# Reordering the steps of a fused attention and token mixer: scores first, weights by casting loads, output weights issued later

## The chip, the cores and the metric

The kernel runs on one core of one Trainium2 chip. The metric is the device time of one execution in microseconds. The kernel before takes 103.31 us (median of three runs, 102.93 to 103.32). The profile's span, from the first to the last instruction, is shorter than the device time of the same run by 1.75 to 3.17 us in the fast runs of the record. Runs over 1.5% above the fastest of the same kernel are called slow and are left out of all comparisons of times.

## The reference

A retention-like attention, block by block with a decaying state, feeds a mixer that works along the sequence. B, H, S, D are 4, 8, 768, 64, the model width is 512, the mixer's inner width 64.

```python
for b in range(nb):                                   # blocks of 64 rows
    intra = np.einsum('bhic,bhjc->bhij', qb, kb) * Dmask[None]
    intra = np.einsum('bhij,bhjd->bhid', intra, vb)
    inter = np.einsum('bhid,bhde->bhie', qb * lam_pow[None], kv_state)
    out[:, :, sl] = intra + inter
    kv_state = lam_block[...] * kv_state + np.einsum('bhsd,bhse->bhde', kb * rev_pow, vb)
...
x = attn_out.transpose(0, 2, 1, 3).reshape(B, S, H * D)
wq, wk = x @ w_q, x @ w_k
mixed = np.einsum('bst,btd->bsd', np.einsum('bsd,btd->bst', wq, wk) / 8, x)
return np.maximum(mixed, 0.0) @ w_out
```

## The kernel before

The work is cut into 16 pairs (a batch and two of its heads), and the main loop has one step per pair. In the text, "the q turn of pair 9" is the group of twelve PE transposes that brings q of pair 9 into the form for the scores. The groups on PE are: q turn, k turn, scores (tile sc), states (tile dps, they need the V scaled by GpSimd, tile vn), inter (tile oa from gs, the copy of the states), values (tile oa from pr), flip (tile xp), and the mixer's wk, wq, py, pm and po. pm multiplies by Y, ScalarE's (ACT's) copy of py; po multiplies by the output weights, wo, and makes the output. In the traces PE's groups run in the program's order.

All loads but the first few and the mixer's small weights are cast from f32 to bf16 by the DMA and are issued by GpSimd, which also scales the V tiles. One pair's loads are these:

```python
def load_more(n):
    load_q(n)                                   # nc.gpsimd.dma_start
    load_kv(n, "k")
    scale_v(n - 2, nc.gpsimd) if n - 2 > 3 else None
    load_kv(n, "v")
...
    load_q(5)
    load_kv(5, "k")
    scale_v(3, nc.gpsimd)
    load_kv(5, "v")
    nc.gpsimd.dma_start(out=wo, in_=moe_w_out.rearrange("(kt p) j -> p kt j", p=128))
    load_more(6)
    load_more(7)
    make_dq(1)
    for n in range(N):
        if 8 <= n + 6 < N:
            load_more(n + 6)
```

So GpSimd's stream holds the output weights (512 KB in bf16) between the loads of pairs 5 and 6. Inside the loop PE's order is:

```python
        if n >= 1 and not (b >= 1 and kk >= 2):
            inter(n - 1)
            scores(n)
        elif n >= 1:
            mix_pm(p, [2 * kk - 4])
            scores(n)
            inter(n - 1)
            mix_pm(p, [2 * kk - 3])
        ...
        masks(n, 0)
        masks(n, 1)
        if n == 4 or n >= 8:
            back()                              # values, flip, po, wk
        if n <= 8:
            states(n)
        ...
        if n <= 8:
            turn(n + 1)                         # q turn, then k turn
        if 8 <= n < N - 1:
            states(n + 1)
```

Of the kernel before, what the change touches and what calls it, by code (L numbers as in the profile page):

```python
# [11 lines left out]
F32 = mybir.dt.float32  # L12
# [7 lines left out]
DHY = 64  # L20
NP = H // 2
# [6 lines left out]
def kernel(  # L28
# [62 lines left out]
    nc.sync.dma_start(out=k0, in_=kv_rows(0, k))  # L91
    q0 = consts.tile([128, 2, 3, 2 * D], F32, name="q0")
    nc.sync.dma_start(out=q0, in_=q_rows(0))
    wqk_f = consts.tile([128, 2, 4, DHY], F32, name="wqk_f")


    nc.scalar.preload_act_table_set("natural_log_exp_and_others")
# [72 lines left out]
    def make_dq(kk):  # L170
        nc.scalar.activation(out=Dq[kk], in_=ET, func=ACT.Exp, scale=lncol[:, kk : kk + 1])
# [5 lines left out]
    wo = consts.tile([128, 4, HD], BF16, name="wo")  # L177

    def load_wqk():

        nc.vector.memset(wqk_f[:, :, 0, 0:1], 0.0)
        for i, w in enumerate((moe_w_q, moe_w_k)):
            nc.sync.dma_start(out=wqk_f[:, i], in_=w.rearrange("(kt p) j -> p kt j", p=128))


    L = defaultdict(dict)
# [2 lines left out]
    def scale_v(n, eng):  # L189
        b, kk = pairs[n]  # L190
        vn = nat.tile([128, 2, NCH, D], BF16, tag="vn", name="vn")
        eng.tensor_tensor(  # L192
            out=vn,
            in0=staged.pop((n, "v")),
            in1=DvI[:, 2 * kk : 2 * kk + 2, :].unsqueeze(3).to_broadcast([128, 2, NCH, D]),
            op=ALU.mult,
        )
        L[n]["vn"] = vn
# [8 lines left out]
    def turn(n):  # L207
        turn_q(n)
        turn_k(n)
# [22 lines left out]
    def turn_k(n):  # L232
        L[n]["kn"] = kn = staged.pop((n, "k"))
        trk = pst([128, S], BF16, "trk")
        for c in range(NCH):
            for hl in range(2):
                nc.tensor.transpose(  # L237
                    trk[hl * 64 : hl * 64 + 64, c * CH : (c + 1) * CH], kn[:, hl, c, :], ident
                )
        kT = tsb.tile([128, S], BF16, tag="kT", name="kT")  # L240
        nc.scalar.copy(out=kT, in_=trk)  # L241
        L[n]["kT"] = kT
# [4 lines left out]
    def states(n):  # L247

        kn, vn = L[n]["kn"], L[n]["vn"]
        dps = pst([128, NCH - 1, D], F32, "dps")  # L250
        for c in range(NCH - 1):
            end = 2 if c < 2 else NCH - 1
            for hl in range(2):
                nc.tensor.matmul(  # L254
                    dps[hl * 64 : hl * 64 + 64, c:end, :],
                    kn[:, hl, c, :],
                    vn[:, hl, c, :].unsqueeze(1).to_broadcast([128, end - c, D]),
                    start=(c == 0),
                    stop=(c == NCH - 2),
                    skip_group_check=True,  # L260
                )
        gs = gsp.tile([128, NCH - 1, D], BF16, tag="gs", name="gs")
        two = gsp.tile([128, 1, D], F32, tag="two", name="two")
        nc.vector.tensor_copy(out=two, in_=dps[:, 1:2, :])
        nc.vector.tensor_copy(out=gs[:, 0:2, :], in_=dps[:, 0:2, :])
        nc.vector.tensor_tensor(
            out=gs[:, 2:, :],
            in0=dps[:, 2:, :],
            in1=two.to_broadcast([128, NCH - 3, D]),
            op=ALU.add,  # L270
        )
        L[n]["gs"] = gs

    def scores(n):
        kT = L[n]["kT"]
        sc = {}
        for a in range(2):
            for hl in range(2):
                sc[a, hl] = pst([128, 3, CH], F32, f"sc{hl}")
            for cc in range(3):  # L280
                c = 3 * a + cc
                for hl in range(2):
                    r = slice(hl * 64, hl * 64 + 64)
                    nc.tensor.matmul(  # L284
                        sc[a, hl][:, cc, :],
                        kT[r, c * CH : (c + 1) * CH],
                        qchunk(n, r, c),
                        start=True,
                        stop=True,
                        skip_group_check=True,  # L290
                    )
        L[n].update(sc=sc, pr={})

    def masks(n, a):
        for hl in range(2):
            t = prb.tile([128, 3, CH], BF16, tag="pr", name="pr")
            nc.vector.tensor_tensor(out=t, in0=L[n]["sc"][a, hl], in1=maskc, op=ALU.mult)  # L297
            L[n]["pr"][a, hl] = t

    def inter(n):  # L300

        gs = L[n]["gs"]
        oa = [pst([128, NCH, D], F32, "oa") for hl in range(2)]
        for c in range(1, NCH):
            for hl in range(2):
                r = slice(hl * 64, hl * 64 + 64)
                nc.tensor.matmul(
                    oa[hl][:, c, :],
                    qchunk(n, r, c),
                    gs[r, c - 1, :],  # L310
                    start=(c == 1),
                    stop=False,
                    skip_group_check=True,
                )
        L[n]["oa"] = oa
# [24 lines left out]
    def flip(n, eng=None):  # L340
        b, kk = pairs[n]
        xp = pst([128, NCH, CH], BF16, "xp")
        for t in range(NCH):
            nc.tensor.transpose(xp[:, t, :], xnat[b][:, t, kk * CH : (kk + 1) * CH], ident)  # L344
        to = xT[b][:, kk, :].rearrange("d (c t) -> d c t", c=NCH)
        if n == N - 1:
            nc.vector.tensor_copy(out=to[:, 0:3], in_=xp[:, 0:3])
            nc.scalar.copy(out=to[:, 3:], in_=xp[:, 3:])
        elif eng is nc.scalar:
            nc.scalar.copy(out=to, in_=xp)  # L350
        else:
            nc.vector.tensor_copy(out=to, in_=xp)
# [146 lines left out]
    warm(2)  # L499
    fq0 = nat.tile([128, 2, 3, 2 * D], BF16, tag="q0", name="fq0")  # L500
    nc.vector.tensor_copy(out=fq0[:, 0], in_=q0[:, 0])
    nc.scalar.copy(out=fq0[:, 1], in_=q0[:, 1])
    staged[0, "q"] = fq0
    turn_q(0)
    scale_v(0, nc.vector)
    scale_v(2, nc.gpsimd)
    load_q(5)
    load_kv(5, "k")
    scale_v(3, nc.gpsimd)
    load_kv(5, "v")  # L510
    nc.gpsimd.dma_start(out=wo, in_=moe_w_out.rearrange("(kt p) j -> p kt j", p=128))
    load_more(6)
    load_more(7)
    make_dq(1)

    for n in range(N):
        b, kk = pairs[n]
        if 8 <= n + 6 < N:
            load_more(n + 6)
        if n + 6 >= N and n + 4 < N:  # L520
            scale_v(n + 4, nc.gpsimd)
        if n == 8:

            late = consts.tile([1, D], BF16, name="late")
            nc.sync.dma_start(out=late, in_=staged[n + 6, "v"][0:1, 0, 0, :])
            store()
        if n == 1:
            load_wqk()
        if n == 4:
            nc.scalar.copy(out=wqk, in_=wqk_f)  # L530
        p = b - 1
        outs = {
            7: [(0, 0), (0, 1), (0, 2)],
            8: [(0, 3), (0, 4)],
            9: [(0, 5)],
            10: [],
            N - 1: [(2, 0)],
        }.get(n)
        if outs is None:
            outs = [[(p - 1, 2), (p - 1, 3)], [(p - 1, 4)], [(p - 1, 5)], [(p, 0), (p, 1)]][kk]  # L540
            outs = [(i, t) for i, t in outs if i >= 0]

        def back():

            if kk == 1 and n > 8:
                flip(n - 2, nc.scalar)
            if n >= 1:
                values(n - 1)
            if n >= 2 and not (kk == 1 and n > 8) and n != 5:
                flip(n - 2, nc.scalar if n < 5 else None)  # L550
            if n == 4:
                flip(n - 1)
            for i, t in outs:
                mix_po(i, t)
            if kk == 1 and n > 8:
                mix_wk(p)


        if n >= 1 and not (b >= 1 and kk >= 2):
            inter(n - 1)  # L560
            scores(n)
        elif n >= 1:
            mix_pm(p, [2 * kk - 4])
            scores(n)
            inter(n - 1)
            mix_pm(p, [2 * kk - 3])
        else:
            scores(n)
        masks(n, 0)
        masks(n, 1)  # L570
        if n == 4 or n >= 8:
            back()

        if n <= 8:
            states(n)
        if n == 5:
            mix_wq(p)
            mix_py(p)
        if n <= 8:
            turn(n + 1)  # L580
        if 8 <= n < N - 1:
            states(n + 1)
        if 8 <= n < N - 2:
            turn(n + 2)
        if n == 0:
            scale_v(1, nc.vector)
            make_dq(2)
        if n == 1:
            make_dq(3)
        if kk == 1 and n > 8:  # L590
            mix_wq(p)
            mix_py(p)
        if n == 4:
            mix_wk(p)
        elif n < 8:
            back()
    bl = B - 1
    inter(N - 1)
    values(N - 1)
    flip(N - 2)  # L600
    mix_po(bl - 1, 1)
    flip(N - 1)
    mix_wk(bl, (0, 1, 2))
# [44 lines left out]
```

## Time and profile before

| | before |
|---|---|
| device time, median | 103.31 us |
| span in the profile | 101.3 us |
| PE, DVE, ACT, POOL busy | 85, 65, 65, 67% of the span |
| states of pair 8 | 48.19 us after the span's start |
| PE's last matmul ends | 97.70 us |

The prediction below shows the lines that bound the kernel. Two more views matter for what follows. The first is the list of DMA issues of the kernel before: tile and source, issuing queue, count, KB each, and the median time in us from issue to landing.

```profile
fv<-in_v_dram POOLq DMA_DIRECT2D x16, 192.0 KB, 5.8
fq<-in_q_dram POOLq DMA_DIRECT2D x15, 192.0 KB, 5.1
fk<-in_k_dram POOLq DMA_DIRECT2D x15, 192.0 KB, 5.7
wo<-in_moe_w_out_dram POOLq DMA_DIRECT2D x1, 512.0 KB, 8.3
```

A q or k load takes 5 to 6 us in the median. The second is PE in two stretches of 3.41 us, with the busy time, the number of matmuls, the granted clock (1.00 is full speed), the DMA share and GB/s:

```profile
42.66:46.07 3.41, 3.36 (x46) 1.00 2.06 151
46.07:49.48 3.41, 3.36 (x59) 1.00 1.85 136
```

In the kernel before, PE has no pause from 42.66 to 49.48 us, because five po groups (three of step 7, two of step 8) and other ready work lie ahead of states 8. Its clock is full.

### The profile page before, as it was taken

What the parts mean: (1) busy time and instruction counts of PE and PEld (TensorE: products, weight loads), DVE (VectorE), ACT (ScalarE), POOL (GpSimd) and SP (SyncE); (2) the same over time, 40 slices, a digit from 0 to 9 for tenths busy, and PEclk for the clock granted to TensorE, in tenths of its full rate; (3) what the DMA queues carried; (4) which work ended last, traced back from release to release, by engine and by line L of the source; (5) the groups of instructions that cost most, each with busy time, mean ns of one, the idle gap of its engine ahead of it and who ended that gap; (6) DMA issues with size and microseconds to landing.
All of it is one profiled execution on the core that took longest, in us unless ns stands there. A gap on an engine that the chain in (4) does not pass through costs nothing.

```text
span 101.3 us, 3514 instructions
## 1 busy us (share of the span) xinstructions
PE 86.3 (85%) x1494; PEld 58.5 (58%) x1504; DVE 65.4 (65%) x165; ACT 65.3 (65%) x127; POOL 67.5 (67%) x69
## 2 busy tenths in 40 slices
PE   4986989768698687999999699999988899999950
PEld 1324778656587564755878375667756466543430
DVE  3153998977699199709786199497746875255330
ACT  5175065666934789676595979676879786568330
POOL 5999999899999399999999999992140000000000
PEclk9999999999999999999999999999999999999999
DMA  0999999999999999999999999999996112523584
GB/s 12 255 181 156 166 166 161 177 157 169 185 187 163 163 172 152 151 154 125 158 133 135 147 123 167 125 140 206 392 400 227 46 69 104 202 108 147 222 309 150
DMA packets 67440, 17.12 MB, mean 169 GB/s; under 512 B 62946, under 2 KB 64482, under 8 KB 67426
## 3 DMA queue, kind: packets, MB, share of 16 engines
q0 software_dynamic: 60400, 9.57, 128.1%
q1 hardware_dynamic: 6882, 7.21, 21.2%
q8 instruction: 11, 0.18, 0.7%
q10 hardware_dynamic: 144, 0.13, 0.4%
q14 instruction: 3, 0.02, 0.1%
HBM read 20.19 MB, written 6.29 MB: 261 GB/s over the span
## 4 chain that ended last, share of the span: by engine, by line
PE 35%; POOL 27%; DMA 17%; ACT 12%; issue 4%; DVE 1%; POOLq 0%; ACTq 0%
PE po L475 14%; DMA fk<-in_k_dram 10%; POOL vn L192 7%; DMA fv<-in_v_dram 7%; POOL fk L78 6%; POOL fv L78 6%; POOL fq L73 5%; ACT rmT L457 5%; PE oa L325 3%; ACT kT L241 3%; PE xp L344 3%; PE dps L254 3%; PE trk L237 3%; PE pm L437 2%; PE trq L218 2%
## 5 line engine op out<-in xcount | busy, mean ns | idle before, releaser
L297 DVE TENSOR_TENSOR pr<-sc,maskc 128x384 bf16<-128x384 f32 x64 | 31.2, 550 | 11.1 <-PE sc L284 11.1
L192 POOL TENSOR_TENSOR vn<-fv,DvI 128x768 bf16<-128x768 bf16 x14 | 21.1, 1506 | 5.8 <-DMA fv<-in_v_dram 4.3
L241 ACT COPY kT<-trk 128x768 bf16<-128x768 bf16 x16 | 12.8, 798 | 16.7 <-PE trk L237 16.7
L475 PE MATMUL po<-wo,rmT 128*128 128x512 bf16 (+1 forms) x90 | 22.7, 370 | 0.6
L485 ACT COPY osb<-po 128x512 f32<-128x512 f32 (+1 forms) x22 | 12.6, 579 | 8.1 <-PE po L475 8.0
L78 POOL DMA_DIRECT2D fv<-in_v_dram x16 | 17.3, 1080 | 0.8 <-POOLq L632 0.8
L78 POOL DMA_DIRECT2D fk<-in_k_dram x15 | 15.7, 1045 | 0.0
L475 PEld LDWEIGHTS <-rmT 128*128 128x128 bf16 x100 | 8.9, 98 | 9.0 <-issue 0.8
L337 ACT CAST xnat<-oa 128x384 bf16<-128x384 f32 x31 | 13.5, 493 | 0.4 <-PE oa L325 0.3
L73 POOL DMA_DIRECT2D fq<-in_q_dram x15 | 12.8, 851 | 0.0
L457 ACT ACTIVATE rmT<-pm 128x384 bf16<-128x384 f32 x28 | 12.2, 499 | 0.4 <-PE pm L437 0.2
L284 PE MATMUL sc<-qT,kT 64*128 64x128 bf16 x192 | 9.8, 228 | 1.8 <-DVE qT L224 0.9
L224 DVE TENSOR_TENSOR qT<-trq,dq 128x768 bf16<-128x768 bf16 x16 | 8.8, 549 | 2.2 <-PE trq L218 2.2
L218 PE MATMUL trq<-ident,fq 128*64 128x128 bf16 x192 | 9.6, 237 | 0.2
L237 PE MATMUL trk<-ident,fk 128*64 128x128 bf16 x180 | 8.3, 231 | 1.6 <-DMA fk<-in_k_dram 1.6
L344 PE MATMUL xp<-ident,xnat 128*128 128x128 bf16 x96 | 8.0, 219 | 0.9 <-ACT xnat L337 0.9
L284 PEld LDWEIGHTS <-kT 64*128 64x128 bf16 x192 | 6.8, 99 | 3.3 <-issue 1.5
L437 PE MATMUL pm<-wqT,Y 64*128 64x384 bf16 x32 | 6.9, 328 | 2.0 <-ACT Y L414 0.9
L254 PE MATMUL dps<-vn,fk 128*64 128x128 bf16 (+2 forms) x150 | 6.9, 224 | 1.7 <-POOL vn L192 1.0
L325 PE MATMUL oa<-vn,pr 128*128 128x64 bf16 x192 | 8.4, 194 | 0.0
L254 PEld LDWEIGHTS <-fk 128*64 128x64 bf16 x150 | 5.4, 113 | 4.8 <-issue 1.4
L325 PEld LDWEIGHTS <-pr 128*128 128x128 bf16 x192 | 6.6, 98 | 2.4 <-issue 1.5
(61 smaller groups left out, 112.6 us busy)
## 6 DMA issues: line engine op xcount, KB each, us to landing
out_dram<-osb SPq DMA_DIRECT2D x23, 256.0 KB, 2.1
fv<-in_v_dram POOLq DMA_DIRECT2D x16, 192.0 KB, 5.8
fq<-in_q_dram POOLq DMA_DIRECT2D x15, 192.0 KB, 5.1
fk<-in_k_dram POOLq DMA_DIRECT2D x15, 192.0 KB, 5.7
wo<-in_moe_w_out_dram POOLq DMA_DIRECT2D x1, 512.0 KB, 8.3
k<-in_k_dram SPq DMA_DIRECT2D x1, 384.0 KB, 3.9
q<-in_q_dram SPq DMA_DIRECT2D x1, 384.0 KB, 4.9
wqk_f<-in_moe_w_q_dram SPq DMA_DIRECT2D x1, 128.0 KB, 6.4
```

The lines of the kernel that those rows point to most:

```text
L73: nc.gpsimd.dma_start(out=t, in_=q_rows(n))
L78: nc.gpsimd.dma_start(out=t, in_=kv_rows(n, dict(k=k, v=v)[nm]))
L192: eng.tensor_tensor(out=vn, in0=staged.pop((n, "v")), in1=DvI[:, 2 * kk : 2 * kk + 2, :].unsqueeze(3).to_broadcast([128, 2, NCH, D]), op=A ...
L241: nc.scalar.copy(out=kT, in_=trk)
L254: nc.tensor.matmul(dps[hl * 64 : hl * 64 + 64, c:end, :], kn[:, hl, c, :], vn[:, hl, c, :].unsqueeze(1).to_broadcast([128, end - c, D]), s ...
L284: nc.tensor.matmul(sc[a, hl][:, cc, :], kT[r, c * CH : (c + 1) * CH], qchunk(n, r, c), start=True, stop=True, skip_group_check=True,)
L297: nc.vector.tensor_tensor(out=t, in0=L[n]["sc"][a, hl], in1=maskc, op=ALU.mult)
L325: nc.tensor.matmul(oa[hl][:, c, :], pr[c // 3, hl][:, c % 3, :], vn[:, hl, c, :], start=False, stop=(c == NCH - 1), skip_group_check=True,)
L337: nc.scalar.copy(out=to, in_=oa[hl])
L457: nc.scalar.activation(out=to, in_=pm, func=ACT.Relu, scale=1.0 / 8.0)
L475: nc.tensor.matmul(po, M[b]["rmT"][:, kt, t * CH : (t + 1) * CH], wo[:, kt, c : c + w], start=(kt == 0), stop=(kt == 3),)
L485: nc.scalar.copy(out=osb[:, c : c + w], in_=po)
```

## The change

The intent is to take waits off PE. In each step the scores come ahead of inter, so that DVE's masks start earlier. In the first half q is turned between the two pairs of masks. The mixer's small weights come by two casting loads on GpSimd in place of plain loads and a cast by ACT. Y is still used in the step after it is made, but now behind that step's scores and inter. The output weights are issued behind nine pairs, with the loads of pair 8 done and those of pair 9 next, and batch 0's po groups start one step later. The diff, cut to its core:

```diff
     def load_wqk():
-        nc.vector.memset(wqk_f[:, :, 0, 0:1], 0.0)
         for i, w in enumerate((moe_w_q, moe_w_k)):
-            nc.sync.dma_start(out=wqk_f[:, i], in_=w.rearrange("(kt p) j -> p kt j", p=128))
+            nc.gpsimd.dma_start(out=wqk[:, i], in_=w.rearrange("(kt p) j -> p kt j", p=128))
...
+    make_dq(1)
+    load_wqk()
     scale_v(2, nc.gpsimd)
...
-    nc.gpsimd.dma_start(out=wo, in_=moe_w_out.rearrange("(kt p) j -> p kt j", p=128))
     load_more(6)
     load_more(7)
...
     for n in range(N):
         if 8 <= n + 6 < N:
             load_more(n + 6)
...
+        if n == 2:
+            nc.gpsimd.dma_start(
+                out=wo, in_=moe_w_out.rearrange("(kt p) j -> p kt j", p=128)
+            )
...
-            7: [(0, 0), (0, 1), (0, 2)],
-            8: [(0, 3), (0, 4)],
-            9: [(0, 5)],
+            8: [(0, 0), (0, 1), (0, 2)],
+            9: [(0, 3)],
+            10: [(0, 4)],
+            11: [(0, 5)],
...
+        if n > 5 and n % 4 in (3, 0):
+            mix_pm((n - 5) // 4, [1 if n % 4 == 3 else 3])
+        scores(n)
+        if n >= 1:
+            inter(n - 1)
+        if n > 5 and n % 4 in (2, 3):
+            mix_pm((n - 5) // 4, [0 if n % 4 == 2 else 2])
         masks(n, 0)
...
+        if n < 10:
+            turn_q(n + 1)
+            masks(n, 1)
             states(n)
+            turn_k(n + 1)
```

Two of the three gs copies also move from DVE to ACT for pairs 0 to 3, and the second half of q0 is cast on DVE in place of ACT.

## The prediction

> **What bounds the kernel now.** I read the page first: the busy shares, then the chain that ended last.
>
> ```profile
> PE 86.3 (85%) x1494; PEld 58.5 (58%) x1504; DVE 65.4 (65%) x165; ACT 65.3 (65%) x127; POOL 67.5 (67%) x69
> ...
> PE 35%; POOL 27%; DMA 17%; ACT 12%; issue 4%; DVE 1%; POOLq 0%; ACTq 0%
> ```
>
> TensorE (PE) is busy for 85% of a 101.3 us span, but the chain is only 35% PE; 27% is GpSimd (POOL) and 17% DMA. So there are at least two regimes. The chain in order of time shows where one gives way to the other (start, length, what):
>
> ```profile
> 23.55 9.91 DMA fk<-in_k_dram
> ...
> 47.75 1.50 POOL vn L192
> ...
> 52.08 1.51 POOL vn L192
> 53.59 0.04 issue
> 53.63 0.42 PE dps L254 x6
> ```
>
> Up to 53.63 us the chain is mostly POOL, which scales a V tile (vn) and issues the next loads in turn, and waits for landings; only from 33.5 to 39.1 is it on PE, ACT and DVE. The last return to POOL is at 52.08; from 53.63 on it holds PE and ScalarE (ACT), short issue gaps, and one DVE piece at the very end. A "states" group (line 254, tile dps) needs the scaled V of its pair, and the trace has PE's groups in the program's order throughout, so everything behind it waits too. The timeline shows these meetings:
>
> ```profile
> 34.76 1.47 POOL L192 TENSOR_TENSOR vn<-fv,DvI 128x768 bf16<-128x768 bf16 x1 [1.52 <-PE pm L437]
> ...
> 40.66 0.42 PE L254 MATMUL dps<-vn,fk 128*64 128x128 bf16 x9 [0.57 <-POOL vn L192]
> ...
> 43.41 1.51 POOL L192 TENSOR_TENSOR vn<-fv,DvI 128x768 bf16<-128x768 bf16 x1
> ...
> 48.19 0.45 PE L254 MATMUL dps<-vn,fk 128*64 128x128 bf16 x10
> ...
> 53.63 0.42 PE L254 MATMUL dps<-vn,fk 128*64 128x128 bf16 x9 [0.23 <-POOL vn L192]
> ```
>
> States of pair 7 (40.66) and of pair 10 (53.63) start just when POOL delivers, after 0.57 and 0.23 us of waiting. States of pair 8 (48.19) start 3.27 us after their vn was ready (43.41 + 1.51 = 44.92), because three output tiles (po) were put ahead of them. The 1.52 us before POOL's scaling at 34.76 are printed as a wait for PE, but that V was issued at 26.00 with 8.6 us to landing, so it landed at 34.6: a DMA wait.
>
> POOL's pace per pair, from the costliest groups: q issue 0.85 + k issue 1.05 + v issue 1.08 + scaling 1.51 = 4.49 us at most (from the scaling at 43.41 to that at 47.75 it is 4.34). Landing times say when the DMAs themselves bind: k takes 5.3 us for pair 1, 9.2 for pair 4, 9.9 for pair 6 (behind the 512 KB of output weights), 5.4 for pair 10. So DMA backlog binds up to about 35 us, POOL to 53.6, PE from there to 97.7; the output's end takes the last 3.6 us.
>
> [...] a 512-column po matmul is listed at 380 ns, yet eight of them take 1.73 us in the chain (67.03 to 68.76), 216 ns each. [...] I therefore count PE work by spacings in the chain, never by busy time. [...] every casting load holds POOL 0.77 to 1.1 us, while the weights' plain loads held only SyncE, 0.37 and 0.51 us. [...]
>
> **The change, part by part.**
>
> *POOL.* Two casting loads of 512 rows each are added before the scaling of pair 2. The output weights, also 512 pieces, cost 0.77; I estimate 0.75 each, +1.5 us. Removed: the 1.52 wait for pair 6 (with the output weights no longer ahead of it, its V should land near 32 us, before POOL asks at about 33.5) and a wait of 0.31 for pair 3. The output weights' own 0.77 moves from before pair 6 to after pair 8. So vn of pair 3 comes at 20.97 + 1.5 - 0.31 = 22.2, pair 6 at 36.23 - 1.1 = 35.1, and from pair 7 on all is 0.3 earlier: pair 8 at 44.6, pair 10 at 53.3. POOL gains almost nothing.
>
> *First half.* Scores first, q turned between the masks, and two of three small gs copies given to ACT for pairs 0 to 3 shorten DVE's loop: today 1.95 (four masks) + 0.68 to 0.85 (gs) + 0.55 (qT), then about 0.5 waiting for the scores. The second half of q0 cast on DVE instead of ACT starts the first scores about 0.5 us earlier. But states of pairs 2 to 8 then stand at POOL's times. From states 5 to states 6, for example, PE has 3.97 us to do (k turn, wq, py, values, scores, inter, one pm pair, q turn, states; spacings below) and POOL takes 35.1 - 30.8 = 4.3; from states 6 to 7 it is 3.07 against 5.2. So steps 0 to 7 gain only waiting time on PE.
>
> *Output tiles.* Batch 0's begin in step 8 instead of 7, as its last pm pair moves there. Hence PE can't fill the wait in step 7: between states 7 and 8 it has k turn 0.35, values 0.46, flip 0.34, pm 0.31, scores 0.34, inter 0.25, q turn 0.34, states 0.38 = 2.77 us for 4.3 us of time. States 8 start at 44.6, and from here on PE is the bound.
>
> *PE work left from states 8*, with spacings from the chain (scores 0.34, inter 0.25, states 0.38, turns 0.69, values 0.46, flip 0.34, po 0.865, wk 0.70, wq 0.77, py 0.78, pm pair 0.31): to states 9, with three po, 5.06; to states 10, with wk, wq, py, two po, 7.22; rest of step 10, 2.14; steps 11 to 15: 3.95, 4.50, 5.58, 3.81, 2.88; tail 16.04, which is today's 14.86 (82.84 to 97.70) plus one pm pair and one po. Sum 51.2 us, so PE can't finish before 44.6 + 51.2 = 95.8. Checked on step 12 of today: sum 4.19, elapsed 4.15 (scores at 65.74 and 69.89).
>
> Today's count from states 8 is 46.4 us from 48.19, and it took 49.5: 3.1 us of stalls. Known among them:
>
> ```profile
> PE pm L437 <- ACT Y L414: 0.9, 2, 0.5
> ...
> PE pm L437 <- ACT Y L420: 0.9, 2, 0.4
> ```
>
> So 1.8 us is waiting for Y. In the new order Y of batch 2 is used after a turn, scores and inter (0.69 + 0.34 + 0.25 = 1.28 us), longer than ACT's three Y copies (0.37 + 0.74): no stall. Batch 1's has only scores and inter ahead, 0.59 us: some 0.6 remains. Another 0.23 of the 3.1 was vn of pair 10. The other 1.05 I keep. Stalls become 0.6 + 1.05 = 1.65, and two po instead of one before the last flip may hide 0.3 in the tail.
>
> *Sum.* 44.6 + 51.2 + 1.65 - 0.3 = 97.1 us against 97.7: 0.6 us earlier. Work that is delayed by one step (4.8 us more left at states 8) eats a 3.6 us earlier start; what is gained is mostly the Y stalls. 103.31 - 0.6 = 102.7.
>
> **Rivals.**
>
> First, the stalls vanish altogether: the wait for Y was the only systematic one in the second half, and both scores and pm would have their operands early. Then 95.8 on PE, 101.4 us. For it: steps 8 and 12 of today run without a stall. Against: ACT serves kT, xnat, rmT, Y and osb in order and is itself busy 65%.
>
> Second, the DMA of the output weights, now beside pair 9's loads, holds up q9, which is turned before states 8. It lengthened landings to 8 to 10 us earlier; at 36 to 45 us the queue is less full (5.7 us for q9 today), so I expect 7 us, which is just in time. At 9 us, states 8 and all behind them move by 1.5 us: 104.2.
>
> Third, buffers: a step now holds four score tiles and two oa tiles before turning q, and the pool has eight PSUM buffers. A bank still held by ACT's or DVE's copy would replace the removed waits; before step 8 POOL's pace hides this, after it the order is nearly the old one. If 0.3 us a step comes back in eight steps, 105.1.
>
> Fourth, the first half was bound by DVE rather than POOL, and everything moves up by 2 to 3 us: 100.5. The starts of states 5, 6, 7 and 10 at POOL's ends speak against it.
>
> **Range and chances.** Centre 102.7. The first rival limits the gain at 101.4 unless POOL itself is faster than I count; the second and third reach 104 to 105. I take 101.1 to 104.7. Faster by over 2% (below 101.2) needs POOL to be ahead of my count as well as no stalls: 0.17. Slower by over 2% (above 105.4) needs a new repeated wait: 0.07. Within 2%: 0.76.
>
> **What would show it.** In the changed profile: POOL's scaling of pair 8 ends at 44.6 within 0.7 us, and states 8 start with it, with PE idle by 1 to 2 us between 36 and 45; the chain leaves POOL for good near 45, not 53.6; pm waits for Y fall from 1.8 to about 0.6 us or less; the wait of 1.52 before pair 6's scaling is gone; scores of pair 15 begin near 78 to 79 and PE's last matmul ends near 97. The prediction is wrong if PE is not held by vn in steps 5 to 8, if q9's landing delays states 8, or if stalls after 45 us differ from 1.65 us by more than 1.5.

One figure is a little narrow: a casting load held GpSimd 0.77 to 1.1 us, but the first load of V 1.20.

## The result, and the profile after

The changed kernel takes 106.48 us (median of four runs, 106.03 to 107.00). The kernel before took 103.19 us in four runs beside it (102.93 to 103.32). The ratio is 1.0324, with a 95% interval of 1.0271 to 1.0377: slower. Ratios here are the mean time of one kernel's fast runs over that of the other's of the same rounds, so they are not quite the ratio of the medians. The prediction of 102.7 us with a range of 101.1 to 104.7 was wrong.

The page of the changed kernel, whose span is 104.4 us (busy shares, the granted clock in 40 slices of 2.6 us, and the chain that ended last by engine):

```profile
PE 85.6 (82%) x1494; PEld 58.2 (56%) x1504; DVE 65.1 (62%) x157; ACT 65.6 (63%) x133; POOL 69.1 (66%) x71
...
PEclk9999999579999999985999999999999999999999
...
PE 43%; POOL 33%; DMA 8%; ACT 7%; issue 4%; DVE 0%; POOLq 0%; ACTq 0%
```

The busy shares hardly moved. Two things are new. The clock of PE dips twice, near slice 8 and near slice 18. In the chain, DMA fell from 17% to 8%, and all of these 8% are one transfer. The chain in order of time shows it (start, length, what):

```profile
36.26 0.76 POOL wo L529
37.02 0.80 POOL fq L73
37.82 8.63 DMA fk<-in_k_dram
46.50 0.85 PE trk L235 x12
47.35 0.76 PE oa L327 x12
```

GpSimd issues the output weights, then q and k of pair 9. k of pair 9 is 8.63 us under way, and the k turn waits for it. The timeline of PE at that place (start, us, line, operation, tile, count, and in brackets the idle time before and what ended it):

```profile
44.39 0.53 PE L216 MATMUL trq<-ident,fq 128*64 128x128 bf16 x12 [0.78 <-DMA fq<-in_q_dram]
44.75 0.44 PE L252 MATMUL dps<-vn,fk 128*64 128x128 bf16 x10
46.50 0.85 PE L235 MATMUL trk<-ident,fk 128*64 128x128 bf16 x12 [1.31 <-DMA fk<-in_k_dram]
47.28 0.82 PE L327 MATMUL oa<-vn,pr 128*128 128x64 bf16 x12
...
52.64 0.42 PE L252 MATMUL dps<-vn,fk 128*64 128x128 bf16 x10
```

The q turn of pair 9 waits 0.78 us, states 8 follow at 44.75, and then PE stands for 1.31 us until k of pair 9 is there. The k turn itself takes 0.85 us, the values 0.82. At full speed a turn takes about 0.5 us, as the q turn above it does. The two stretches shown for the kernel before explain it:

```profile
42.66:46.07 3.41, 1.50 (x38) 1.00 2.27 164
46.07:49.48 3.41, 2.76 (x32) 0.50 2.26 163
```

PE is busy for only 1.50 of 3.41 us in the first, and in the second its clock is halved. In the trace's clock records of the same run, each of the two halvings lasts 3413 ns, and they start 27306 ns apart, which is eight times 3413. The full clock between them lasts 23893 ns, seven times 3413, and behind them 54613, sixteen times. So the changes of the clock in this trace lie on a grid of 3.413 us (the halvings in the other traces fit such a grid too), and 42.66 to 46.07 is one square of it. The halving before it, from 18.76 to 22.17 us, follows a square with 1.46 us of matmul time. There PE waits for GpSimd's vn anyway, with 2.05 us idle before states 2.

On GpSimd, the wait of 1.52 us ahead of the scaling of pair 6 is gone, and pair 8's follows without one:

```profile
33.77 1.50 POOL L190 TENSOR_TENSOR vn<-fv,DvI 128x768 bf16<-128x768 bf16 x1
...
43.19 1.50 POOL L190 TENSOR_TENSOR vn<-fv,DvI 128x768 bf16<-128x768 bf16 x1
```

### The profile page after: what moved, and what is told of

It reads as the page before. It is cut to its first block, busy times and chain, and to the rows that moved or that the text cites. A ratio compares the mean times of both kernels' runs of the same rounds, so it can differ in the third digit from the quotient of the medians.

```text
span 104.4 us, 3514 instructions
## 1 busy us (share of the span) xinstructions
PE 85.6 (82%) x1494; PEld 58.2 (56%) x1504; DVE 65.1 (62%) x157; ACT 65.6 (63%) x133; POOL 69.1 (66%) x71
## 4 chain that ended last, share of the span: by engine, by line
PE 43%; POOL 33%; DMA 8%; ACT 7%; issue 4%; DVE 0%; POOLq 0%; ACTq 0%
PE po L477 19%; DMA fk<-in_k_dram 8%; POOL fk L78 8%; POOL vn L190 7%; POOL fv L78 7%; POOL fq L73 7%; PE oa L327 4%; PE xp L346 4%; PE trk L235 2%; PE pm L439 2%; ACT kT L239 2%; ACT rmT L459 2%; PE dps L252 2%; PE wq L387 2%; PE py L407 2%
## 5 line engine op out<-in xcount | busy, mean ns | idle before, releaser
L299 DVE TENSOR_TENSOR pr<-sc,maskc 128x384 bf16<-128x384 f32 x64 | 32.0, 548 | 6.5 <-PE sc L286 6.4
L190 POOL TENSOR_TENSOR vn<-fv,DvI 128x768 bf16<-128x768 bf16 x14 | 21.1, 1510 | 2.7 <-DMA fv<-in_v_dram 2.7
L286 PE MATMUL sc<-qT,kT 64*128 64x128 bf16 x192 | 9.1, 221 | 2.5 <-ACT kT L239 1.3
L252 PE MATMUL dps<-vn,fk 128*64 128x64 bf16 (+2 forms) x150 | 6.9, 222 | 3.6 <-POOL vn L190 3.3
L216 PE MATMUL trq<-ident,fq 128*64 128x128 bf16 x192 | 8.5, 222 | 1.5 <-DMA fq<-in_q_dram 0.8
L286 PEld LDWEIGHTS <-kT 64*128 64x128 bf16 x192 | 6.2, 96 | 5.0 <-issue 2.1
L327 PE MATMUL oa<-vn,pr 128*128 128x64 bf16 x192 | 8.9, 200 | 0.0
L346 PE MATMUL xp<-ident,xnat 128*128 128x128 bf16 x96 | 8.7, 231 | 0.0
L327 PEld LDWEIGHTS <-pr 128*128 128x128 bf16 x192 | 7.1, 102 | 2.7 <-issue 2.2
L216 PEld LDWEIGHTS <-fq 128*64 128x64 bf16 x192 | 6.1, 110 | 3.4 <-DMA fq<-in_q_dram 1.2
```

Of the source, the lines that this page charges most:

```text
L190: eng.tensor_tensor(out=vn, in0=fv, in1=DvI[:, 2 * kk : 2 * kk + 2, :].unsqueeze(3).to_broadcast([128, 2, NCH, D]), op=ALU.mult,)
L216: nc.tensor.transpose(trq[hl * 64 : hl * 64 + 64, 2 * a : 2 * a + 2, r, :], fq[:, hl, a, r * D : (r + 1) * D], ident,)
L252: nc.tensor.matmul(dps[hl * 64 : hl * 64 + 64, c:end, :], kn[:, hl, c, :], vn[:, hl, c, :].unsqueeze(1).to_broadcast([128, end - c, D]), s ...
L286: nc.tensor.matmul(sc[a, hl][:, cc, :], kT[r, c * CH : (c + 1) * CH], qchunk(n, r, c), start=True, stop=True, skip_group_check=True,)
L299: nc.vector.tensor_tensor(out=t, in0=L[n]["sc"][a, hl], in1=maskc, op=ALU.mult)
L327: nc.tensor.matmul(oa[hl][:, c, :], pr[c // 3, hl][:, c % 3, :], vn[:, hl, c, :], start=False, stop=(c == NCH - 1), skip_group_check=True,)
```

## The experiments

The first theory after the result was that the output weights directly ahead of pair 9's loads cost all of the excess, by the wait for k of pair 9 and by the halved clock. The rivals were that a PE with less work in the first half loses its clock by itself, and that the new order of the steps or the casting weight loads cost time.

**e1_wo_back.** The changed kernel with the output weights at their old place.

```diff
+    nc.gpsimd.dma_start(out=wo, in_=moe_w_out.rearrange("(kt p) j -> p kt j", p=128))
     load_more(6)
...
-        if n == 2:
-            nc.gpsimd.dma_start(out=wo, ...)
```

> The changed kernel with the output weights' load back ahead of pair 6. My theory: behind pair 8 it lengthened the landing of pair 9's k to 8.6 us, so the k turn of pair 9 stood 1.3 us after states 8, and this with the wait for q9 and vn lowered PE's clock to half for 3.4 us. Here k9 should land near 43 us, before states 8 at 44.7, and the 1.3 us wait goes; if the half-speed stretch from 45.2 us goes too, the time falls by 2.8 us to about 103.7; if it stays (PE still waits for vn of pair 8), by 1.3 us to about 105.2. Rival (the new order of the groups itself costs, in PSUM waits): stays at 106 or above.

Two of its four runs were fast: 103.87 and 103.97 us. The ratio is 1.0126 (1.0091 to 1.0160), so more than half of the 3.2% came back, but not all. The profiled run took 134.1 us at a clock of 0.555 for 112.6 us on end and says nothing about the kernel; the fourth was slow, 106.83.

**e2_warm.** The changed kernel with eleven more matmuls on zeros, to keep PE busy.

```diff
         if n > 5 and n % 4 in (2, 3):
             mix_pm((n - 5) // 4, [0 if n % 4 == 2 else 2])
+        if n in (7, 8):
+            warm(3)
...
             states(n)
+            if n == 8:
+                warm(5)
```

> The changed kernel with 11 dummy matmuls on zeros put into PE's waits of steps 7 and 8 (3 before the q turn of each, 5 between states 8 and the k turn of pair 9), which cost no more than the waits they stand in. My theory: the wait for k9 stays, but PE keeps its full clock from 45 to 49 us: about 1.5 us less, 105.0. Rival (the lost time is the DMA wait alone, the clock is a consequence without cost): 106.5 unchanged. If the clock drops although PE is kept busy, the dummies are not what the clock counts.

This failed as a test. In its profile, of a slow run, q of pair 9 itself came late: PE stood for 2.76 us ahead of the q turn, and the five dummy matmuls that stand behind that turn in the program started only at 48.24 us:

```profile
46.97 0.85 PE L216 MATMUL trq<-ident,fq 128*64 128x128 bf16 x12 [2.76 <-DMA fq<-in_q_dram]
```

The square of the clock's grid from 42.84 to 46.26 held 1.25 us of matmul time, and the clock was halved for the next two squares. Only one of four runs counts as fast (104.79), so there is no ratio.

**e3_wo_back_warm.** Both edits, e1 and e2.

> Both edits together: output weights ahead of pair 6, and the 11 dummy matmuls. My theory: no wait for k9 and full clock after 45 us; the count on record then holds, about 103.0 (its own figure was 102.7). Some of the dummies may stand in the way now, since k9 is there at once: up to 1.1 us more, 104.1. Rival of the order itself costing: 105 to 106.

Its fast runs took 106.22 and 107.08 us, ratio 1.0489 (1.0433 to 1.0545). The profile has no halving from about 17 us to PE's end and no wait for k of pair 9. But q of pair 6 now waits 1.56 us and k of pair 6 0.54, and the dummy matmuls stand in the way: states 8 start at 46.10, the k turn of pair 9 at 47.64. The dummy work cost time here: the fast runs of e1, which is the same without it, took 103.87 and 103.97 us.

**e4_wqk_sp.** The changed kernel with the mixer's weights loaded as before, by SyncE with a cast on ACT.

```diff
-            nc.gpsimd.dma_start(out=wqk[:, i], ...)
+            nc.sync.dma_start(out=wqk_f[:, i], ...)
...
+        if n == 4:
+            nc.scalar.copy(out=wqk, in_=wqk_f)
```

> The changed kernel with the mixer weights loaded as before, plainly from SyncE with a cast on ScalarE. My theory: GpSimd is freed of two issues of 0.75 us, so vn of pairs 2 to 8 and all loads from pair 5 on come 1.5 us earlier; the half-speed stretch near 18 us goes (PE no longer waits 2 us for vn of pair 2); the wait for k9 stays. About 105.0. Rival (DMAs bind, not GpSimd's issue): no change, 106.5.

Three of four runs count as slow (106.06 to 106.70, beside a 104.25), so no ratio is given, and the times decide nothing. The profile, of a slow run, shows where PE waits. GpSimd is ahead and states 8 start 0.65 us earlier, at 44.10. The k turn of pair 9 starts at 46.21, no more than 0.29 earlier. The wait grew by what was won:

```profile
46.21 0.53 PE L238 MATMUL trk<-ident,fk 128*64 128x128 bf16 x12 [1.66 <-DVE gs L271]
```

The releaser printed is DVE's gs, which doesn't feed this group. The list of DMA issues settles it: k of pair 9 was issued at 37.18 us and took 9.0 to landing, so it landed at 46.2, where the gap ends. It is the same wait. The square 43.84 to 47.25 held 1.70 us of matmul time, and the next was halved. So the wait and the halving stay without the two casting loads on GpSimd. That these loads do not make the loss is shown by e5 and e9 below, which keep them.

**e5_quarter_wo.** The changed kernel with only a quarter of the output weights loaded. Its output is wrong, which doesn't matter for the time. All groups and their order stay.

```diff
-                    wo[:, kt, c : c + w],
+                    wo[:, 0, c : c + w],
...
-                out=wo, in_=moe_w_out.rearrange("(kt p) j -> p kt j", p=128)
+                out=wo[:, 0:1], in_=moe_w_out.rearrange("(kt p) j -> p kt j", p=128)[:, 0:1]
```

> The changed kernel with only a quarter of the output weights loaded, in the same place behind pair 8, and used for all four (a wrong result on purpose). Nothing else moves: PE, DVE and ACT have the same instructions. My theory (384 KB of the load's own traffic beside pair 9 is what holds k9): k9 lands near 44.5 to 45 instead of 46.5, PE waits at most 0.3 us for it and keeps its clock after 45 us; 103.5 to 104. If k9 lands early but the clock still drops, about 105. Rival (the order costs, not the load): 106 or above.

It took 103.67 us (103.53 to 104.31), ratio 1.0030 (0.9964 to 1.0097). All four runs had full clock. The timeline of PE at the same place, and then the two stretches:

```profile
44.44 0.42 PE L252 MATMUL dps<-vn,fk 128*64 128x128 bf16 x9 [0.67 <-POOL vn L190]
...
44.72 0.50 PE L235 MATMUL trk<-ident,fk 128*64 128x128 bf16 x11
45.15 0.52 PE L327 MATMUL oa<-vn,pr 128*128 128x64 bf16 x12
...
49.48 0.42 PE L252 MATMUL dps<-vn,fk 128*64 128x128 bf16 x10
```

```profile
42.66:46.07 3.41, 2.67 (x68) 1.00 2.02 147
46.07:49.48 3.41, 3.36 (x45) 1.00 1.81 139
```

The k turn follows states 8 without a wait, and the clock stays full (the stretches are those of the changed kernel's grid). From states 8 to states 9 it takes 5.04 us in place of 7.89. That is the whole excess over this kernel: to PE's end the two need 53.11 and 55.96 us from states 8, 2.85 apart, and 7.89 - 5.04 is 2.85. This shows that the transfer of the output weights ahead of pair 9 is the cause (bytes and pieces, which this run cuts together), and that the new order of the steps costs no more than the interval leaves open.

**e6_before_wo9.** The kernel before with the output weights at the new place.

```diff
-    nc.gpsimd.dma_start(out=wo, in_=moe_w_out.rearrange("(kt p) j -> p kt j", p=128))
     load_more(6)
...
+        if n == 2:
+            nc.gpsimd.dma_start(out=wo, ...)
```

> The kernel before with only one part of the change: the output weights behind pair 8. My theory: in the old order the k turn of pair 9 comes after two more output tiles, at 48.6, so a landing at 46.5 holds nothing; pair 6's k and V land 1.5 to 2 us earlier; the first output tile (42.4) may wait up to 1 us for the weights. 102 to 103, same as before, and no wait for k9. Rival (the load behind pair 8 is bad in any order): 104 or more.

The fast runs took 103.70, 104.85 and 104.76 us; ratio 1.0092 (0.9998 to 1.0186), a little above what was expected; one slow run was left out. There is no wait for q or k of pair 9, because this order turns both only after states 8, at 49.24 and 49.58 us. The old order tolerates the late landing; the new order, which turns q ahead of states 8 and reaches its k turn at 45, doesn't. k of pair 9 was 9.2 us under way here too, from 37.79 to about 47.0. The first po group starts at 43.16 (42.40 before) after a wait of 0.87 us: the output weights themselves, issued at 36.22 and 6.9 us under way, landed only then.

**e7_po_early.** The changed kernel with the output weights at the old place and batch 0's po groups and last pm one step earlier.

```diff
-            8: [(0, 0), (0, 1), (0, 2)],
+            7: [(0, 0), (0, 1), (0, 2)],
...
+        if n == 7:
+            mix_pm(0, [3])
```

> The changed kernel with the output weights ahead of pair 6 and batch 0's output tiles and last pm pair one step earlier (three in step 7), as in the kernel before, to fill PE's wait for vn of pair 8. My count: 48.3 us of PE work from states 8, which start near 47; 102.0 to 102.5, at or a little below the kernel before, and the clock full after 40 us. Rival (the rest of the new order costs 3 us): 105 or more.

The fast runs took 103.36 and 104.79 us (two were slow), ratio 1.0058 (0.9927 to 1.0188), which decides nothing. The profile, of a slow run, shows a wait where I look for the rest of e1's loss:

```profile
33.26 0.53 PE L216 MATMUL trq<-ident,fq 128*64 128x128 bf16 x12 [3.03 <-DMA fq<-in_q_dram]
```

At the old place the output weights stand ahead of pair 6's loads, and the new order asks for q of pair 6 earlier than the old one did (at 30.2 us here; the old order's q turn ran at 32.03 without a wait). The square 30.61 to 34.02 held 0.76 us of matmul time, and the next was halved.

**e8_wo_back_again.** e1 once more, as its trace could not be read.

> The first experiment again, since its profile fell into an execution whose clock was 0.56 from 17 us on. Expected like its two undisturbed timed runs: 103.9. PE waits for q6 and k6 in step 5 (together 1 to 2 us) in place of k9, states 8 near 45.3, no wait for k9; a half-speed stretch between 40 and 50 us in some executions, which then take 106 to 107.

Three of the four runs count as slow beside one of 103.63 us, so no ratio. The profile, again of a slow run and with a clock of 0.95 outside the halvings, shows the same wait as e7's:

```profile
32.10 0.53 PE L216 MATMUL trq<-ident,fq 128*64 128x128 bf16 x12 [1.96 <-DMA fq<-in_q_dram]
```

e3's profile, of a fast run, has it too (1.56 us). No wait for k of pair 9 is left. Both places for one load of 512 KB give the new order a wait, at pair 6 or at pair 9.

**e9_wo_paced.** The changed kernel with the output weights as four plain loads from SyncE, one per step in steps 3 to 6, each held back by a small write of DVE, and cast by ACT two steps later.

```diff
+    wo_f = consts.tile([128, 4, HD], F32, name="wo_f")
+    def load_wo(i):
+        nc.vector.memset(wo_f[:, i, 0:1], 0.0)
+        nc.sync.dma_start(out=wo_f[:, i], in_=moe_w_out[i * 128 : (i + 1) * 128, :])
...
+        if 3 <= n < 7:
+            load_wo(n - 3)
+        if 5 <= n < 9:
+            nc.scalar.copy(out=wo[:, n - 5], in_=wo_f[:, n - 5])
```

> The changed kernel with the output weights loaded plainly from SyncE in four pieces of 256 KB, one at each of steps 3 to 6, each cast on ScalarE two steps later. My theory: the same bytes, spread over about 15 us in which landings took 4.1 to 5.0 us, delay no pair's q or k beyond its use; GpSimd loses one issue of 0.77 us. No wait over 0.5 us for q9 or k9, clock full from 22 us on, states 8 near 44; 103.0, the same as or slightly under the kernel before. Rival (any 1 MB of extra reads in this stretch costs the same wherever it stands): 105 to 106.

It took 103.44 us (103.12 to 103.71), ratio 1.0031 (0.9989 to 1.0073), with right results. The full weights are loaded, yet no q or k turn waits for its load. The square that holds states 8 and the one after it:

```profile
42.35:45.77 3.42, 2.56 (x72) 1.00 2.18 159
45.77:49.18 3.41, 3.36 (x42) 1.00 2.02 152
```

States 8 are at 44.62, states 9 at 49.66. It also lost its clock for 6.8 us, but from 18.4 us on, where GpSimd sets the pace: that cost nothing visible, as the profiled run took 103.71 us and the two runs at full clock 103.18 and 103.70.

**e10_wo_wqk_paced.** e9 with the mixer's weights loaded by SyncE too (the edit of e4).

> As the last, and the mixer weights too as in the kernel before, from SyncE with a cast on ScalarE. If GpSimd's program holds states 2 to 8, as I count, they come 1.5 us earlier still (states 8 near 42.5) and the end with them: 101.5 to 102. Rival (behind GpSimd the DMAs stand at once, as the fourth experiment hinted): states 8 at 43.5 or later and 103.

It took 103.57 us (103.25 to 104.02), ratio 1.0050 (0.9999 to 1.0100). Taking 1.5 us of issue time off GpSimd did not bring the scaled V tiles forward, because GpSimd then waits for the V loads (start, us, and the wait in brackets):

```profile
24.41 1.47 POOL L199 TENSOR_TENSOR vn<-fv,DvI 128x768 bf16<-128x768 bf16 x1 [0.89 <-DMA fv<-in_v_dram]
29.67 1.47 POOL L199 TENSOR_TENSOR vn<-fv,DvI 128x768 bf16<-128x768 bf16 x1 [0.92 <-DMA fv<-in_v_dram]
```

vn of pair 5 is ready at 31.14 us, against 30.93 in e9. I read this as two limits of nearly the same height up to here, GpSimd and the DMAs, so that freeing one gains nothing. PE also waits for k of pair 4, 0.95 us, and for q and k of pair 6, 0.50 and 0.29, which it did not in e9.

**e11_all_paced_po_early.** e10 with the pieces in steps 2 to 5, cast in steps 4 to 7, and e7's earlier po groups.

> As the last (pieces one step earlier), and batch 0's output tiles and last pm pair one step earlier, to fill PE's waits between states 7 and 8. Count: 2.9 us of work moved into a wait of some 1.5 us, so 1.5 us better than the last: 100 to 100.5, faster than both kernels. Rival: the first output tile waits for the weights' cast, or DMAs hold the states: 102 to 103.

It took 103.99 us (103.62 to 104.57), ratio 1.0091 (1.0043 to 1.0139). It was expected at 100 to 100.5. The q turn of pair 4 waits 1.48 us for its load and the k turn 1.12, and the clock is halved once behind them; states 8 start at 47.23, where e13 below has them at 45.74. PE's end is 97.72, where e9's is 97.73: the late start ate what the earlier po groups gained. How much of it the pieces make by coming one step earlier is not separated: e4, which has the mixer's weights on SyncE and no pieces, waits 0.99 and 0.73 us at the same place.

**e12_before_wo_paced.** The kernel before with the output weights in four pieces from SyncE at steps 2 to 5, cast in steps 4 to 7.

> The kernel before with the output weights loaded in the same four pieces from SyncE at steps 2 to 5. Pair 6's k (9.9 us to landing today) and V are no longer held: states 6 and 7 come 1 to 1.5 us earlier, 102 to 102.5. If the new order of the groups is worth something by itself, the last run is faster than this one by over 1 us; if not, the two are alike.

It took 105.37 us (104.54 to 105.70), ratio 1.0208 (1.0151 to 1.0265), called unclear as the interval crosses 2%; 102 to 102.5 was expected. Here pacing harms: GpSimd waits 2.8 us for V of pairs 3 to 5, the clock is halved twice, and states 8 start at 50.46. Whether the step of the pieces or the order of the loop makes this, no run separates.

**e13_wo_paced_po_early.** e9 with the casts one step after each piece, and e7's earlier po groups and pm.

> The ninth experiment's kernel (output weights in four paced pieces, mixer weights by casting loads as in the change) with batch 0's output tiles and last pm pair one step earlier. There states 8 started at 44.6 with PE having waited before them, and the end came 53.1 us later. My account: 2.9 us of work moves ahead of states 8, about half of it into the waits of steps 6 to 8; states 8 near 46.3, end of PE near 96.4 instead of 97.7, 102.0 to 102.3, 1% under the kernel before. Rival (the empty time before states 8 cost nothing but the clock): 103.4, as the ninth.

In five timed rounds its median is 102.81 us; its five fast runs took 102.14 to 103.04 (the sixth was slow, 105.81), ratio 0.9974 (0.9935 to 1.0014). That is level with the kernel before, a quarter of a per cent under it within the noise, and the fastest version found. The pauses near states 8 are filled with po:

```profile
40.80:44.21 3.41, 3.36 (x49) 1.00 2.19 161
44.21:47.62 3.41, 3.36 (x80) 1.00 2.11 146
```

States 8 start at 45.74 and PE ends at 96.22 us.

## Why the prediction was wrong

**GpSimd: right.** The two casting weight loads took 1.50 us, as estimated. vn of pair 6 was ready at 33.77 + 1.50 = 35.27 us (35.1 predicted), that of pair 8 at 43.19 + 1.50 = 44.69 (44.6), of pair 10 at 53.34 (53.3). The wait of 1.52 us is gone.

**First half: right.** States 8 began at 44.75 (44.6 predicted), and the chain leaves GpSimd for good at 37.8 us, earlier than the 45 foretold, since it goes over to the load of k. PE was busy for 6.84 of the 9 us from 36 to 45, so idle for 2.2, just over the 1 to 2 foretold. One reading of the prediction's was off, without a consequence for its sum: it has three po groups ahead of the old kernel's states 8, and there are five.

**PE from states 8: the term that failed.** The path is told by five times (us from the span's start):

| | before | after | e5 | e9 | e13 |
|---|---|---|---|---|---|
| states 8 | 48.19 | 44.75 | 44.44 | 44.62 | 45.74 |
| k turn of pair 9 | 48.81 | 46.50 | 44.72 | 44.90 | 45.99 |
| states 9 | 49.30 | 52.64 | 49.48 | 49.66 | 49.03 |
| states 10 | 53.63 | 60.49 | 57.33 | 57.52 | 56.89 |
| PE's end | 97.70 | 100.71 | 97.55 | 97.73 | 96.22 |

The prediction's sum has 5.06 us from states 8 to states 9. The changed kernel took 7.89; e5, with a quarter of the weights' bytes, took 5.04. So the count of PE's work was right for this stretch, and two costs were missing from it. One of the prediction's own signs of being wrong came true with them: from states 8 to PE's end the stalls were 55.96 - 51.2 = 4.8 us, not within 1.5 of 1.65.

The first cost is the wait for k of pair 9. The failing step is the second rival: "it holds up q9, which is turned before states 8 ... I expect 7 us, which is just in time". q of pair 9 did land after 7.4 us (37.01 to 44.39), and states 8 were not delayed. But k of pair 9, issued 0.81 us after q, landed only after 8.63 us, and in the new order is needed right behind states 8. The rival followed only the load in front. Measured from states 8, the k turn starts 1.75 us later in the changed kernel and 0.28 in e5: 1.47 us.

The second cost is the half clock. From the k turn to states 9 the changed kernel needs 52.64 - 46.50 = 6.14 us, e5 49.48 - 44.72 = 4.76: 1.38 us. It was in no rival; the step "from here on PE is the bound" took PE's speed for given. I take it for a consequence of the waits: q's 0.78 us and the greater part of k's 1.31 fall into one square of the clock's grid, which then holds 1.50 us of matmul time; the same stretch of e5 holds 2.67. The rival that the emptier first half alone brings the halving doesn't stand: e5 and e9 have the same emptier first half and keep their clock here.

The two make 2.85 us. The remaining difference is small: states 8 were 0.15 late, and the stalls behind them, where I counted 1.65 - 0.3 = 1.35, were 53.11 - 51.2 = 1.9 in e5. Together with 2.85 that is 3.55 of the 3.6 us by which PE's end missed 97.1.

**Waits for Y: right in kind, off in size.** This view lists what PE waited for: us in total, times, longest.

```profile
PE trk L235 <- DMA fk<-in_k_dram: 1.3, 1, 1.3
...
PE pm L439 <- ACT Y L422: 0.4, 1, 0.4
PE pm L439 <- ACT kT L239: 0.4, 1, 0.4
```

The waits of pm for Y fell from 1.8 to 0.4 us (0.6 predicted). But 0.4 for ACT's kT copy took the place of one of them, as the argument against the first rival said that it might.

**The third and fourth rivals** find no support. A PSUM wait in every step would have shown in e5 as well, which needs 21.1 us from states 10 to the end of states 15's group, 1.1 more than counted and without a wait that returns in every step. States 4, 5, 7 and 8 still start within 0.1 us of GpSimd's delivery, which speaks against the fourth.

**Why nothing was gained even without the fault.** e5 and e9 are level with the kernel before, as the prediction's sum had it for the change itself (0.6 us earlier, 0.15 measured in e5's end of PE). States 8 come 3.6 us earlier in e9, but the five po groups that used to stand ahead of them now lie behind them. e13 takes three of these back, and puts a pm pair one step earlier, and ends PE 1.5 us earlier than e9.

**What stays open.** Why e12 lost what e9 did not was not separated. Nor was what makes e9 work: it changes the spacing, the issuing queue (SyncE) and the place of the cast (ACT) at once. The clocks of 0.555 in e1's profiled run, for 112.6 us, and 0.95 in e8's have no explanation here; with the first, the profile lists a po matmul at 559 ns in the mean, against 370 in the kernel before. And the link from waits to half clock rests on the agreement of all traces (last section), not on a run that changed the wait and held the rest.

## What to carry to other kernels

When a large load moves, follow every load behind it in the queue to its first use, not only the next one, and look at where the new order has moved that use; here a load cut into pieces between the steps (e9) did what one block at either end could not, though in the old order (e12) the pieces did harm. The waits for q and k of pair 9 (0.78 and 1.31 us), on a PE that is otherwise the bound, came with two costs: the later k turn (1.47 us) and, as far as these traces tell, the half clock (1.38). Work that fills a wait is worth something only while the wait is there: moving it behind gave the time back here (in e9 states 8 came 3.6 us earlier, and PE's end stayed at 97.73 us, against 97.70).

## What the traces show of the clock and of the loads

- In the traces of the 15 kernels, 15 halvings came after a square at or near full speed and before PE's end; each lasted one, two or three squares of 3413 ns and began on their grid. The squares ahead of 13 of them held 0.76 (e7) to 1.70 us (e4) of matmul time, the other two 2.00 (e2) and 2.15 (e12). The emptiest square that was not followed by a halving held 1.86 us (the changed kernel, 8.52 to 11.94 us). So the matmul time of the square ahead doesn't separate the two sharply in these records, whose matmul ends are modelled. In the changed kernel, ahead of the halving at 46.07 us, the longest pause inside the square was 0.9 us, and PE had 1.50 of 3.41 us of matmul time.
- With 512 KB in one load ahead of it, k of pair 9 landed after 8.63 us. With a quarter of the bytes (e5) no q or k turn waited for its load, and with four spaced pieces from SyncE (e9) none did either; with the pieces one step earlier and the mixer's weights on SyncE (e11) q and k of pair 4 waited, 1.48 and 1.12 us.
